# Seven block products for the second product of two token groups, and all weight operands kept in DRAM

## The chip, the cores and the metric

The kernel runs on one core of a Trainium2 chip. The metric is the device time of one execution in microseconds; the median of the runs is the figure to be predicted. TensorE is called PE here, VectorE DVE, ScalarE ACT, GpSimd POOL, and SyncE SP; SP issues nearly all DMAs. One execution was also profiled; its span runs from the first to the last instruction on the core.

## What is computed

Linear attention gives 2304 rows of 512 features. A gated feed-forward layer maps them to 2304 x 512 again. Then eight experts with router weights P (from eight rounds of row and column scaling of `exp(x @ w_gate)`) are summed, and this last stage is what the change touches:

```python
out = np.zeros((N, D), dtype=np.float32)
for e in range(E):
    h = np.maximum(x @ w1[e], 0.0)
    ye = h @ w2[e]
    out += P[:, e:e + 1] * ye
```

N is 2304, D 512, E 8, and h has 1024 columns for each expert. Everything is fp32. Each operand is split into a high part, rounded to the matmul's own type, and a low part (the rest); a product is then three matmuls: high by high, high by low, low by high.

## The kernel before

The last stage cuts the tokens into three groups of 768 (`GROUPS`), and each group into two halves of 384 (`NT`). For each group, the eight experts are worked off in four slices of 256 columns of h, so a group has 32 *units* and the stage 96. Unit n belongs to group 0, 1 or 2 in the code; in words these are groups one, two and three.

**First product of a unit** (`m2_burst`, `m2_m1`, `m2_product`, line 1162). The 256 x 512 slice of w1 and the 512 x 768 tokens are taken as 2 x 2 blocks, and Strassen's scheme in Winograd's form makes the four result blocks from seven block products, called M1 to M7 in the code (`PRODUCTS`). Its weight side needs A11, A12, A22 and four sums S1 to S4; its token side B11, B21, B22 and four sums T1 to T4. Each of the seven is six matmuls of 128 x 128 weights by 384 columns, so 42 in all. They run through two PSUM banks (`sbank`, tiles sb). DVE adds the pieces together (line 1238), ACT applies the relu and makes the high part (line 1176), DVE the low part (line 1179).

**Second product** (`m2_second`, `m2_s2`, lines 1192 to 1194). Here h is the weight side: for each of six token tiles of 128 there are six matmuls of 512 columns, 36 in all, summed over the four units of an expert in six PSUM banks (tiles yb). After the fourth unit `m2_evac` multiplies each bank by the router weight of its tokens and adds it to acc or accx (line 1211); after the last expert it stores the rows.

**Weights.** `load_unit` loads 512 KB of w1 and 512 KB of w2 for a unit (tiles rw). `prep` forms the four sums on DVE, and the high (ACT) and low (DVE) parts of the seven operands (tiles u, from the pool `wp` of nine slots), and those of w2. `prep_tick` does one step of that at a time, between the pieces of other work. For units 0 and 1 the finished operands are also written to DRAM (`keep`, tiles kept), and the first two units of the other groups read them back (`prep_kept`).

**Order.** Nothing schedules this work: each engine runs its instructions in the order in which the code issues them, and so does SP with its DMAs, each waiting at the queue's head for its semaphores. While a unit's second product runs, DVE prepares the next unit's weights; at the end of a group the functions called through `later` build the next group's token operands (`operands`, tiles op).

## Time and profile before

| what | us |
|---|---|
| median of 3 runs | 2058.14 |
| lowest and highest run | 2057.95, 2060.36 |
| span of the profiled execution | 2056.3 |
| PE busy | 2036.7 (99%) |
| DVE busy | 1328.5 (65%) |
| ACT busy | 821.1 (40%) |
| POOL busy | 142.8 (7%) |

The span is read with the busy shares only as a first look: matmuls are pipelined, so a busy PE says that it always has a matmul in flight, and not how fast they follow. The rhythm has to be taken from the start times. The last stage fills the time from about 556 us to the end.

### The profile page before, as it was taken

How to read it: one execution, taken by the hardware profiler on the slowest of the kernel's cores; microseconds unless marked ns; L12 is line 12 of the kernel's file. 1: busy time of each engine (PE TensorE's matmuls, PEld its weight loads, DVE VectorE, ACT ScalarE, POOL GpSimd, SP SyncE). 2: the span in 40 equal slices, each digit the busy share in tenths (PEclk: the TensorE clock that was granted, in tenths of full speed). 3: DMA queues.
4: the chain of work that ended last, by engine and by line, in shares of the span. 5: the costliest groups of instructions: out<-in, count | busy, mean ns of one | idle time of the engine just before them, and what ended most of it. 6: DMA issues, size and time to landing. Idle time of an engine off the chain costs nothing.

```text
span 2056.3 us, 26589 instructions
## 1 busy us (share of the span) xinstructions
PE 2036.7 (99%) x10391; PEld 1811.7 (88%) x10391; DVE 1328.5 (65%) x2660; ACT 821.1 (40%) x1603; POOL 142.8 (7%) x162
## 2 busy tenths in 40 slices
PE   8899999999999999999999999999999999999999
PEld 7788888887898999999899899899899989989988
DVE  7865753543678667667666667766666666666774
ACT  5644532322444434334334434433434533433442
POOL 4532211111100000000000000000000000000000
PEclk9999999999999999999999999999999999999999
DMA  9400310110222221221252222222134221122220
GB/s 270 127 24 21 103 53 30 52 58 10 77 72 63 82 62 62 74 70 62 69 177 62 65 80 62 66 79 62 62 107 139 62 81 63 62 74 70 62 71 32
DMA packets 108357, 153.24 MB, mean 75 GB/s; under 512 B 5832, under 2 KB 72392, under 8 KB 107464
## 3 DMA queue, kind: packets, MB, share of 16 engines
q1 hardware_dynamic: 107960, 151.43, 23.2%
q8 instruction: 81, 1.33, 0.3%
q14 instruction: 44, 0.36, 0.1%
q10 hardware_dynamic: 272, 0.13, 0.0%
HBM read 141.05 MB, written 10.49 MB: 74 GB/s over the span
## 4 chain that ended last, share of the span: by engine, by line
PE 96%; DVE 1%; POOL 0%; ACT 0%; issue 0%; DVEq 0%
PE sb L1162 34%; PE yb L1194 13%; PE yb L1193 13%; PE yb L1192 13%; PE pg L801 2%; PE y L803 2%; PE pv L801 2%; PE y L802 2%; PE y L801 2%; PE pg L802 2%; PE pg L803 2%; PE pv L802 2%; PE pv L803 2%; PE kv L458 1%; PE xp L543 1%; PE lg L894 0%
## 5 line engine op out<-in xcount | busy, mean ns | idle before, releaser
L1244 ACT COPY cs<-sb 128x384 f32<-128x384 f32 x96 | 46.1, 480 | 551.7 <-PE sb L1162 551.7
L1238 DVE TENSOR_TENSOR u<-mc,sb 128x384 f32<-128x384 f32 x96 | 53.1, 553 | 305.8 <-PE sb L1162 305.8
L1193 PE MATMUL yb<-u,hw 128*128 128x512 f32 x576 | 225.4, 391 | 0.0
L1194 PE MATMUL yb<-u,hw 128*128 128x512 f32 x576 | 225.2, 391 | 0.0
L1194 PE MATMUL yb<-u,hq 128*128 128x512 f32 x576 | 225.0, 391 | 0.0
L1193 PE MATMUL yb<-u,hq 128*128 128x512 f32 x576 | 224.5, 390 | 0.0
L1192 PE MATMUL yb<-u,hw 128*128 128x512 f32 x576 | 224.3, 389 | 0.0
L1192 PE MATMUL yb<-u,hq 128*128 128x512 f32 x576 | 223.9, 389 | 0.0
L1238 DVE TENSOR_TENSOR cs<-u,sb 128x384 f32<-128x384 f32 x288 | 159.1, 553 | 85.3 <-PE sb L1162 84.0
L1176 ACT ACTIVATE hq<-cs 128x384 fp32r<-128x384 f32 x192 | 100.9, 526 | 200.7 <-DVE cs L1238 200.7
L1162 PE MATMUL sb<-op0T,u 128*128 128x384 f32 x768 | 144.5, 336 | 0.4 <-DVE u L1238 0.4
L1162 PE MATMUL sb<-op2T,u 128*128 128x384 f32 x768 | 144.3, 335 | 0.0
L1162 PE MATMUL sb<-op1T,u 128*128 128x384 f32 x768 | 144.3, 335 | 0.0
L1162 PEld LDWEIGHTS sb<-op0T,u 128*128 128x128 f32 x768 | 134.8, 188 | 3.0 <-DVE u L1238 0.7
L1162 PEld LDWEIGHTS sb<-op2T,u 128*128 128x128 f32 x768 | 134.9, 188 | 2.5
L1162 PEld LDWEIGHTS sb<-op1T,u 128*128 128x128 f32 x768 | 134.9, 188 | 2.5
L1192 PEld LDWEIGHTS yb<-u,hq 128*128 128x128 f32 x576 | 108.2, 188 | 23.8
L1193 PEld LDWEIGHTS yb<-u,hq 128*128 128x128 f32 x576 | 108.0, 188 | 23.6
L1194 PEld LDWEIGHTS yb<-u,hw 128*128 128x128 f32 x576 | 108.1, 188 | 22.8
L1194 PEld LDWEIGHTS yb<-u,hq 128*128 128x128 f32 x576 | 108.1, 188 | 22.7 <-DVE hq L1179 0.4
L1069 DVE TENSOR_TENSOR u<-rw,u 128x512 fp32r<-128x512 f32 x184 | 125.5, 683 | 1.2 <-ACT u L1060 1.2
L1193 PEld LDWEIGHTS yb<-u,hw 128*128 128x128 f32 x576 | 108.1, 188 | 19.5
(244 smaller groups left out, 4151.4 us busy)
## 6 DMA issues: line engine op xcount, KB each, us to landing
rw<-in_moe_w_dram SPq DMA_DIRECT2D x184, 512.0 KB, 3.6
u<-kept SPq DMA_DIRECT2D x8, 896.0 KB, 4.6
raw<-in_moe_w_gate_dram SPq DMA_DIRECT2D x10, 512.0 KB, 3.7
raw<-in_moe_w_val_dram SPq DMA_DIRECT2D x10, 512.0 KB, 3.7
k<-in_k_dram SPq DMA_DIRECT2D x8, 512.0 KB, 5.2
acc<-in_q_dram SPq DMA_DIRECT2D x8, 512.0 KB, 8.6
v<-in_v_dram SPq DMA_DIRECT2D x16, 256.0 KB, 6.8
raw<-in_moe_w_out_dram SPq DMA_DIRECT2D x8, 512.0 KB, 3.5
```

The source lines that it names most:

```text
L458: nc.tensor.matmul(kv[:, (h - h0) * 2 * DV : (h - h0 + 1) * 2 * DV], lhsT=kk.rearrange("p c d -> p (c d)"), rhs=vv, start=(u == 0 and h == ...
L801: nc.tensor.matmul(o, lhsT=w(0), rhs=xb[0], start=first, stop=False)
L802: nc.tensor.matmul(o, lhsT=w(0), rhs=xb[1], start=False, stop=False)
L803: nc.tensor.matmul(o, lhsT=w(1), rhs=xb[0], start=False, stop=last)
L1069: tt(out=w2[:, 1, f], in0=r2[:, f], in1=w2[:, 0, f].bitcast(F32), op=ALU.subtract)
L1162: nc.tensor.matmul(bank[:, 0:NT], lhsT=w[wz][:, WI[wname], c, :], rhs=x[:, xz, c, :], start=(start and c == 0 and j == 0), stop=(c == 1 an ...
L1176: nc.scalar.activation(out=h[:, 0], in_=src, func=AF.Relu)
L1192: nc.tensor.matmul(py, lhsT=h[:, 0, s], rhs=w2[:, 0, f], start=(u == 0 and f == 0), stop=False)
L1193: nc.tensor.matmul(py, lhsT=h[:, 0, s], rhs=w2[:, 1, f], start=False, stop=False)
L1194: nc.tensor.matmul(py, lhsT=h[:, 1, s], rhs=w2[:, 0, f], start=False, stop=(u == UE - 1 and f == 1))
L1238: add = lambda o, a, b: nc.vector.tensor_tensor(out=o, in0=a, in1=b, op=ALU.add)
L1244: nc.scalar.copy(out=c11, in_=px)
```

## The change

Group one keeps its form, with its seven first products in another order (M1, M2, M6, M5, M7, M4, M3), two of the sums replaced by ACT copies out of PSUM, and two of the six second-product tiles run inside the next unit's first product. `prep` becomes `prep_first` (w1) and `prep_second`, which now also forms the sums of w2's blocks and seven operands of them. Every unit of group one writes all its operands to DRAM (`keep`: 4 x 896 KB), and the units of groups two and three only read them back (`recall`).

In groups two and three the second product is made by seven block products as well, and transposed: w2 is the weight side, and the result has 128 features by 384 tokens. The router weight must then be in h. So `probs_out` writes P, transposed, to DRAM, `probs_in` reads an expert's row back, broadcast to all partitions (`pb0`, or a part of acc1), and `half_mul` does relu and product in one DVE instruction. `m2_p1(n)` is the first product of unit n and `m2_p2(n - 1)`, called after it, the second product of the unit before. A block is three matmuls of 384 columns. M2, M3 and M4 stay in the six banks yb over a whole group (`m2_stay`); M1, M5, M6 and M7 go in turn through the two banks sb (`m2_turn`), and DVE adds each into SBUF (`m2_fold`, tiles in acc0 and acc1). The differences T1 to T4 of h (`sum_of`) and the low parts (`lo`) wait in a list, `pend`, from which `pop` issues them at fixed places. `m2_p2_last` closes a group: it adds the products together, PE transposes 24 blocks back (`turned_part`), and `turned_out` stores the rows.

At the end of group one the operands of group two are built as before; at the end of group two those of group three are built inside `m2_p2(62)` and `m2_p2_last(63)`, with their sums on POOL.

The core of the diff:

```diff
+    def keep(n, k, pair):
+
+        for z, t in enumerate(pair):
+            kept[n, k, z] = d = dp.tile([P, KW], F32, name=f"kept{n}_{k}_{z}")
+            t = t.bitcast(F32)
+            if k == 0:
+                nc.sync.dma_start(out=d, in_=t[:, 0:KW])
+            else:
+                nc.sync.dma_start(out=d[:, 0 : 2 * P], in_=t[:, 0 : 2 * P])
+                nc.sync.dma_start(out=d[:, 2 * P : KW], in_=t[:, 4 * P : 2048])
...
+    def recall(n, k):
...
+        pair = slots(f"u{n}_{k}")
+        for z, t in enumerate(pair):
+            nc.sync.dma_start(out=t[:, 0:KW].bitcast(F32), in_=kept[n % PER, k, z])
+        if k == 0:
+            w1s[n] = first_view(pair)
+        else:
+            w2s[n] = pair
...
+    def prep_second(n):
+
+        r2 = unit_raw.pop((n, 1)).rearrange("p f e -> p (f e)")
+        a11, a21, a12, a22 = (r2[:, z * 256 : (z + 1) * 256] for z in range(4))
+        sums = sp.tile([P, 1024], I32, tag="raw", name=f"t{n}", bufs=RAWS).bitcast(F32)
+        s1, s2, s3, s4 = (sums[:, z * 256 : (z + 1) * 256] for z in range(4))
+        pair = w2s[n] = slots(f"u{n}_1")
+        hi, lo = pair
...
+        tt(out=s3, in0=a11, in1=a21, op=ALU.subtract)
+        tt(out=s4, in0=a12, in1=s2, op=ALU.subtract)
+        cp(out=hi[:, 1024:1536], in_=sums[:, 0:512])
+        yield
+        tt(out=lo[:, 0:1024], in0=r2, in1=hi[:, 0:1024].bitcast(F32), op=ALU.subtract)
+        cp(out=hi[:, 1536:2048], in_=sums[:, 512:1024])
+        yield
+        tt(out=lo[:, 1024:1536], in0=sums[:, 0:512], in1=hi[:, 1024:1536].bitcast(F32), op=ALU.subtract)
+        yield
+        tt(out=lo[:, 1536:2048], in0=sums[:, 512:1024], in1=hi[:, 1536:2048].bitcast(F32), op=ALU.subtract)
+        keep(n, 1, pair)
+
...
-        m2_product(n, "M5", x, True)
-        add(c22, u2, px)
-        low22 = m2_relu(n, 1, 1, c22)
-        low11()
+        m2_product(n, "M5", y, True)
+        m2_low(0, 0, c11)
         mid(2)
-        m2_product(n, "M4", y, False)
-        add(c21, u1, py)
-        low21 = m2_relu(n, 1, 0, c21)
+        m2_product(n, "M7", x, False)
+        nc.scalar.copy(out=u2, in_=px)
         mid(3)
-        m2_product(n, "M3", x, False)
-        add(c12, u1, px)
-        low12 = m2_relu(n, 0, 1, c12)
-        low21()
+        add(c22, u2, py)
+        m2_relu(1, 1, c22)
+        m2_product(n, "M4", x, False)
+        nc.scalar.copy(out=c21, in_=px)
+        m2_low(1, 1, c22)
+        m2_relu(1, 0, c21)
         mid(4)
-        low12()
-        low22()
-
...
+    def probs_in(g, e):
...
+            return
+        t = pb_place[(g * E + e) % 2]
+        d = state["pd"].rearrange("(t e) p -> t e p", e=E)
...
+            src = d[4 * b + j : 4 * b + j + n, e, :]
+            nc.sync.dma_start(
+                out=t[:, at * P : (at + n) * P].rearrange("p (t q) -> p t q", t=n), in_=src.partition_broadcast(P)
+            )
...
+    def half_mul(n, name, c):
+        g, e, u = units[n]
+        z = int(name[2]) - 1
+        nc.vector.scalar_tensor_tensor(
+            out=fb[name],
+            in0=c,
+            scalar=0.0,
+            in1=pbc[g, e][:, z * NT : (z + 1) * NT],
+            op0=ALU.max,
+            op1=ALU.mult,
+        )
+
+    def hi(n, name):
+        nc.scalar.copy(out=hop[n][name][:, 0], in_=fb[name])
+
+    def lo(n, name):
+        h = hop[n][name]
+        nc.vector.tensor_tensor(out=h[:, 1], in0=fb[name], in1=h[:, 0].bitcast(F32), op=ALU.subtract)
+
+    def sum_of(n, name):
+        x, y = {"T1": ("B12", "B11"), "T2": ("B22", "T1"), "T3": ("B22", "B12"), "T4": ("B21", "T2")}[name]
+        nc.vector.tensor_tensor(out=fb[name], in0=fb[x], in1=fb[y], op=ALU.subtract)
+        hi(n, name)
+
+    pend = []
...
+    def m2_p1(n):
+
+        old = ring["old"]
...
+        add = lambda o, a, b: nc.vector.tensor_tensor(out=o, in0=a, in1=b, op=ALU.add)
+        m1, u1 = mt[:2]
+        m5 = m1
+        m2_product(n, "M1", x, True)
+        nc.scalar.copy(out=m1, in_=px)
+        pop(2)
+        m2_product(n, "M2", y, True)
+        pop(1)
+        m2_product(n, "M6", x, False)
+        add(fb["B11"], m1, py)
+        nc.scalar.copy(out=u1, in_=px)
+        half_mul(n, "B11", fb["B11"])
+        m2_product(n, "M5", y, True)
+        nc.scalar.copy(out=m5, in_=py)
+        hi(n, "B11")
+        pop(2)
+        m2_product(n, "M7", x, False)
+        pop(len(pend))
+        add(fb["B22"], m5, px)
+        half_mul(n, "B22", fb["B22"])
+        hi(n, "B22")
+        m2_product(n, "M3", y, False)
+        m2_product(n, "M4", x, False)
+        add(fb["B12"], u1, py)
+        half_mul(n, "B12", fb["B12"])
+        half_mul(n, "B21", px)
+        hi(n, "B21")
+        for name in ("T3", "T1", "T2", "T4"):
+            pend.append(lambda name=name: sum_of(n, name))
+        for name in ("B11", "B22", "B21", "T1", "T2", "T3", "T4"):
+            pend.append(lambda name=name: lo(n, name))
+
...
+    def m2_mm(n, name, j, bank, start):
+
+        wname, hname = PRODUCTS[name]
+        w, h = w2s[n], hop[n][hname]
+        d = slice(WI[wname] * 2 * P + j * P, WI[wname] * 2 * P + (j + 1) * P)
+        for k, (wz, hz) in enumerate(((0, 0), (0, 1), (1, 0))):
+            nc.tensor.matmul(
+                bank[:, 0:NT], lhsT=w[wz][:, d], rhs=h[:, hz], start=(start and k == 0), stop=True, skip_group_check=True
+            )
...
+    def m2_stay(n, name, j):
+        m2_mm(n, name, j, ybank[2 * ("M2", "M3", "M4").index(name) + j], n % PER == 0)
...
+    def m2_turn(n, name, j, bank):
+        m2_mm(n, name, j, bank, True)
+
+    def m2_fold(n, name, j, bank):
+        a = macc[name, j]
+        if n % PER == 0:
+            nc.vector.tensor_copy(out=a, in_=bank[:, 0:NT])
+        else:
+            nc.vector.tensor_tensor(out=a, in0=bank[:, 0:NT], in1=a, op=ALU.add)
...
+    def m2_p2(n, work):
+
+        y, x = sbank
+        m2_stay(n, "M3", 0)
+        m2_turn(n, "M1", 0, x)
+        m2_stay(n, "M2", 0)
+        m2_turn(n, "M1", 1, y)
+        m2_fold(n, "M1", 0, x)
+        m2_stay(n, "M2", 1)
+        pop()
+        m2_turn(n, "M5", 0, x)
+        m2_fold(n, "M1", 1, y)
+        pop()
+        work(0)
+        m2_turn(n, "M5", 1, y)
+        m2_fold(n, "M5", 0, x)
+        m2_stay(n, "M4", 0)
+        pop()
+        m2_turn(n, "M6", 0, x)
+        m2_fold(n, "M5", 1, y)
+        work(1)
+        m2_turn(n, "M6", 1, y)
+        m2_fold(n, "M6", 0, x)
+        pop()
+        work(2)
+        m2_stay(n, "M3", 1)
+        m2_turn(n, "M7", 0, x)
+        m2_fold(n, "M6", 1, y)
+        m2_turn(n, "M7", 1, y)
+        m2_fold(n, "M7", 0, x)
+        work(3)
+        m2_stay(n, "M4", 1)
+        m2_fold(n, "M7", 1, y)
...
+    def m2_p2_last(n, work, later):
...
+        for k, m in ((1, 2), (6, 2), (5, 3), (7, 3)):
+            name = f"M{k}"
+            m2_turn(n, name, 0, x)
+            m2_turn(n, name, 1, y)
+            m2_stay(n, f"M{m}", int(k in (6, 7)))
+            for j, bank in ((0, x), (1, y)):
+                m2_fold(n, name, j, bank)
+            for j in range(2):
+                if k == 6:
+                    add(A(6, j), A(1, j), A(6, j))
+                elif k == 5:
+                    add(A(5, j), A(5, j), A(6, j))
+                elif k == 7:
+                    add(A(6, j), A(6, j), A(7, j))
+                    add(A(7, j), A(7, j), A(5, j))
             work(k)
-            if k % 2:
-                next(state["steps"], None)
+        finals = [lambda z=z, k=k, j=j: add(A(k, j), R(z, j), A(k, j)) for z, k in ((2, 1), (3, 5), (4, 6)) for j in range(2)]
+        if later:
+            pend.extend(finals)
+        else:
+            for f in finals[0:4]:
+                f()
+        m2_stay(n, "M4", 0)
+        m2_stay(n, "M4", 1)
+        if not later:
+            for f in finals[4:6]:
+                f()
+            for i in range(3, 6):
+                turned_part(i, 1, 1, rows_bank[i])
+
...
+    def turned_out(g, i, ps, eng):
+
+        b, j = gtiles[g][i]
+        o = [acc[2], acc[3]][i // 4][:, i % 4, :]
+        eng(out=o, in_=ps)
+        nc.sync.dma_start(out=out_rows(b, j), in_=o)
...
+    pb_place = [pb0[:, 0 : 2 * NT], flat[1][:, 3 * NT : 5 * NT]]
+    probs_in(1, 0)
...
+    ORDER2 = ["oB11", "oB21", "T1", "oT1", "T2", "oT2", "oT3", "T4", "oT4", "oB22"]
+    later = operands(2, ORDER2, temp2, lambda name: mt[int(name[-1])])
...
+    for n in range(PER, last + 1):
+        g, e, u = units[n]
+        start = n % PER == 0
+        if u == 1:
+            probs_in(*((g, e + 1) if e < E - 1 else (g + 1, 0)))
+        if start and g > 1:
+            m2_p2(n - 2, lambda k: (flush(k), next(later)))
+            m2_p2_last(n - 1, lambda k: [next(later, None) for _ in range(2)], True)
+            assert next(later, None) is None
+            m2_p1(n)
+            for i in range(6):
+                for d in range(2):
+                    turned_part(i, d, i // 3, ybank[i])
+                turned_out(g - 1, i, ybank[i], nc.vector.tensor_copy if i % 3 == 1 else nc.scalar.copy)
+            pop(6)
+        elif start:
+            m2_p1(n)
+            pop(6)
+        else:
+            m2_p1(n)
+            if not (g < len(GROUPS) - 1 and n % PER == PER - 1):
+                m2_p2(n - 1, flush if n == last else idle)
+        recall(n + 2, 0)
+        recall(n + 1, 1)
+    rows_bank = [ybank[0], ybank[1], ybank[3], sbank[0], sbank[1], ybank[2]]
```

**Where instructions stand: DVE in the steady unit of group two or three.** Before, at the end of unit 39, the preparation of unit 41's weights stands in a row with the evacuations of an expert of group two (s and u are weight tiles, rw the loaded weights, yb the PSUM banks):

```order
L1049 TENSOR_TENSOR s41_9683<-rw41_0_9564,s41_9683 128x256 [waits DVE_49]
L1211 SCALAR_TENSOR_TENSOR acc1_106<-yb0_4814,probs_104,acc1_106 128x512 [waits PE_49]
L1052 TENSOR_TENSOR u41_1_9681<-rw41_0_9564,u41_0_9680 128x512 [waits Activation_49]
L1211 SCALAR_TENSOR_TENSOR acc1_106<-yb1_4815,probs_104,acc1_106 128x512 [waits PE_49]
L1055 TENSOR_TENSOR u41_1_9681<-rw41_0_9564,u41_0_9680 128x256 [waits Activation_49]
L1211 SCALAR_TENSOR_TENSOR accx_4820<-yb2_4816,probs_104,accx_4820 128x512 [waits PE_49]
```

After, in the second product of a unit of group three (acc0 and acc1 hold the folded products, sb the two PSUM banks, mt2, acc4 and fy1 the differences T3, T1 and T2, T4 of h; L1408 is the fold and L1330 the difference):

```order
L1408 TENSOR_TENSOR acc0_105<-sb0_4674,acc0_105 128x384 [waits PE_49]
L1330 TENSOR_TENSOR mt2_9362<-fx_9356,fy1_9358 128x384 [waits DVE_49]
L1408 TENSOR_TENSOR acc0_105<-sb1_4675,acc0_105 128x384 [waits PE_49]
L1330 TENSOR_TENSOR acc4_109<-fy1_9358,fx_9356 128x384
L1408 TENSOR_TENSOR acc0_105<-sb0_4674,acc0_105 128x384 [waits PE_49]
L1330 TENSOR_TENSOR acc4_109<-fx_9356,acc4_109 128x384 [waits DVE_49]
L1408 TENSOR_TENSOR acc0_105<-sb1_4675,acc0_105 128x384 [waits PE_49]
L1408 TENSOR_TENSOR acc0_105<-sb0_4674,acc0_105 128x384 [waits PE_49]
L1330 TENSOR_TENSOR fy1_9358<-fy0_9357,acc4_109 128x384 [waits DVE_49]
L1408 TENSOR_TENSOR acc1_106<-sb1_4675,acc1_106 128x384 [waits PE_49]
L1408 TENSOR_TENSOR acc1_106<-sb0_4674,acc1_106 128x384 [waits PE_49]
L1408 TENSOR_TENSOR acc1_106<-sb1_4675,acc1_106 128x384 [waits PE_49]
```

The weights have left DVE; eight folds stand there now, with the four differences set between them.

**Where instructions stand: SP at the end of group one.** Before, the operands of unit 33 (u, from kept) are read back around the first stores of the group:

```order
L1006 DMA u33_0_8697<-kept1_0_4708 128x1792 [waits DMAHW3_49,PE_49]
L1007 DMA u33_1_8698<-kept1_1_4710 128x1792 [waits DVE_49,PE_49]
L995 DMA rw34_0_8701<-in_moe2_w1_dram 128x4x256 [waits DMAHW5_49,DVE_49]
L995 DMA rw34_1_8703<-in_moe2_w2_dram 128x2x512 [waits DMAHW7_49,DMAHW6_49,DVE_49]
L1219 DMA out_0_dram<-acc0_105 128x512 [waits DVE_49]
L1219 DMA out_0_dram<-acc0_105 128x512 [waits DMAHW0_49,DVE_49]
L1013 DMA u33_2_8764<-kept1_2_4712 128x2048 [waits DMAHW1_49,PE_49,Pool_49]
```

After, the last two of the group's six stores, two operand pairs, and the router weights of group two (pd is P in DRAM, pb0 its place in SBUF):

```order
L1226 DMA out_0_dram<-accx_4828 128x512 [waits DMAHW2_49,DVE_49]
L1226 DMA out_0_dram<-accx_4828 128x512 [waits DMAHW3_49,DVE_49]
L1016 DMA u32_1_0_9339<-kept0_1_0_4630 128x1792 [waits DMAHW4_49,PE_49]
L1016 DMA u32_1_1_9340<-kept0_1_1_4633 128x1792 [waits DMAHW5_49,PE_49]
L1016 DMA u33_0_0_9343<-kept1_0_0_4808 128x1792 [waits DMAHW6_49,PE_49]
L1016 DMA u33_0_1_9344<-kept1_0_1_4810 128x1792 [waits DMAHW7_49,PE_49,Pool_49]
L1303 DMA pb0_9359<-pd_7227 128x2x128 [waits DMAHW3_49,DMAHW2_49,DMAHW0_49]
L1303 DMA pb0_9359<-pd_7227 128x128 [waits DMAHW1_49]
```

The read of the router weights now stands behind the six stores and four reads of 896 KB, and it is what DVE's first product of group two needs.

**Where instructions stand: DVE at the end of group two.** Before, in unit 63, the operands of group three (op2) stand between the evacuations:

```order
L1114 TENSOR_TENSOR op2B21_12606<-acc2_107,op2B21_12606 128x2x256 [waits Activation_49]
L1114 TENSOR_TENSOR op2B21_12606<-acc3_108,op2B21_12606 128x2x128 [waits Activation_49]
L1211 SCALAR_TENSOR_TENSOR acc1_106<-yb0_4814,probs_104,acc1_106 128x512 [waits PE_49]
L1114 TENSOR_TENSOR op2T3_12619<-t2T3_12498,op2T3_12619 128x768 [waits Activation_49]
L1211 SCALAR_TENSOR_TENSOR acc1_106<-yb1_4815,probs_104,acc1_106 128x512 [waits PE_49]
L1114 TENSOR_TENSOR op2T1_12630<-long0_4821,op2T1_12630 128x768 [waits Activation_49]
```

After, in the last two second products of group two, between the folds, with their sums made by POOL:

```order
L1326 TENSOR_TENSOR hb_9348<-mt2_9362,hb_9348 128x384
L1326 TENSOR_TENSOR hb_9348<-fy1_9358,hb_9348 128x384 [waits Activation_49]
L1408 TENSOR_TENSOR acc1_106<-sb0_4674,acc1_106 128x384 [waits PE_49]
L1408 TENSOR_TENSOR acc1_106<-sb1_4675,acc1_106 128x384 [waits PE_49]
L1116 TENSOR_TENSOR op2T1_13453<-acc2_107,op2T1_13453 128x2x256 [waits Activation_49]
L1116 TENSOR_TENSOR op2T1_13453<-acc2_107,op2T1_13453 128x2x128 [waits Activation_49]
L1408 TENSOR_TENSOR acc1_106<-sb0_4674,acc1_106 128x384 [waits PE_49]
L1408 TENSOR_TENSOR acc0_105<-sb1_4675,acc0_105 128x384 [waits PE_49]
L1408 TENSOR_TENSOR acc0_105<-sb0_4674,acc0_105 128x384 [waits PE_49]
L1116 TENSOR_TENSOR op2T2_13475<-acc2_107,op2T2_13475 128x2x256 [waits Activation_49]
L1116 TENSOR_TENSOR op2T2_13475<-acc2_107,op2T2_13475 128x2x128 [waits Activation_49]
L1408 TENSOR_TENSOR acc0_105<-sb1_4675,acc0_105 128x384 [waits PE_49]
```

The operand copies now stand among folds of the two banks through which PE turns.

## Rows read from the trace of the kernel before

**Rows 1.** The core's span, us, and its mean granted TensorE clock

```profile
core 0: 2056.3 us, clock 0.999
```

**Rows 2.** The page's chain that ended last: share of the span by engine

```profile
PE 96%; DVE 1%; POOL 0%; ACT 0%; issue 0%; DVEq 0%
```

**Rows 3.** That chain's pieces in time: start us, us, engine, tile, line, instructions

```profile
609.18 7.30 PE sb L1162 x42
...
1043.76 7.30 PE sb L1162 x42
...
1075.28 7.30 PE sb L1162 x42
```

**Rows 4.** Waits: engine line <- waited for: us in all, times, longest us

```profile
PE sb L1162 <- DVE cs L1238: 0.4, 2, 0.2
```

**Rows 5.** DVE in time, 900 to 914: start us, us, line, op, out<-in, [idle before<-releaser]

```profile
900.02 0.69 DVE L1062 TENSOR_TENSOR u<-s,u 128x512 fp32r<-128x512 f32 x1
900.63 0.68 DVE L1069 TENSOR_TENSOR u<-rw,u 128x512 fp32r<-128x512 f32 x1
...
908.35 0.55 DVE L1238 TENSOR_TENSOR cs<-u,sb 128x384 f32<-128x384 f32 x1 [0.49 <-PE sb L1162]
908.82 0.55 DVE L1179 SCALAR_TENSOR_TENSOR hw<-cs,hw 128x384 fp32r<-128x384 f32 x1
...
912.52 0.42 DVE L1044 TENSOR_TENSOR s<-rw 128x256 f32<-128x256 f32 x1
912.97 0.42 DVE L1045 TENSOR_TENSOR s<-s,rw 128x256 f32<-128x256 f32 x1
913.32 0.42 DVE L1048 TENSOR_TENSOR s<-rw 128x256 f32<-128x256 f32 x1
```

**Rows 6.** PE and DVE in time, near 563 and 905, in the same columns

```profile
562.55 0.55 DVE L1238 TENSOR_TENSOR u<-mc,sb 128x384 f32<-128x384 f32 x1
...
563.15 3.42 PE L1162 MATMUL sb<-op0T,u 128*128 128x384 f32 x18 [0.36 <-DVE u L1238]
...
905.03 1.20 PE L1162 MATMUL sb<-op0B,u 128*128 128x384 f32 x6
905.23 0.55 DVE L1238 TENSOR_TENSOR u<-mc,sb 128x384 f32<-128x384 f32 x1 [3.92 <-PE sb L1162]
```

**Rows 7.** Page, groups by line: busy us, mean ns | idle before, its releaser

```profile
L1244 ACT COPY cs<-sb 128x384 f32<-128x384 f32 x96 | 46.1, 480 | 551.7 <-PE sb L1162 551.7
...
L1238 DVE TENSOR_TENSOR cs<-u,sb 128x384 f32<-128x384 f32 x288 | 159.1, 553 | 85.3 <-PE sb L1162 84.0
...
L1162 PEld LDWEIGHTS sb<-op0T,u 128*128 128x128 f32 x768 | 134.8, 188 | 3.0 <-DVE u L1238 0.7
```

**Rows 8.** Stretches: us, busy by engine (instructions), granted clock, DMA share, GB/s

```profile
core 0: us, PE busy (x) PEld busy (x) DVE busy (x) ACT busy (x) POOL busy (x), PEclk, DMA share, GB/s
453.00:460.00 7.00, 7.00 (x33) 5.79 (x32) 4.04 (x8) 1.79 (x4) 1.30 (x1) 1.00 0.88 330
1030.00:1032.00 2.00, 2.00 (x14) 2.00 (x13) 1.06 (x2) 1.00 (x2) 0.00 (x0) 1.00 0.90 369
```

**Rows 9.** DMA issues: out<-in, queue, count, KB each, median us to landing

```profile
u<-kept SPq DMA_DIRECT2D x8, 896.0 KB, 4.6
...
acc<-in_q_dram SPq DMA_DIRECT2D x8, 512.0 KB, 8.6
...
out_dram<-accx SPq DMA_DIRECT2D x6, 256.0 KB, 3.0
```

**Rows 10.** DVE and SP in time, the last 7 us

```profile
2052.27 0.75 DVE L1211 SCALAR_TENSOR_TENSOR acc<-yb,probs,acc 128x512 f32<-128x512 f32 x1 [0.61 <-PE yb L1194]
...
2053.05 0.33 SPq L1219 DMA_DIRECT2D out_dram<-acc  x1
```

**Rows 11.** Groups by line and shape, POOL and PE

```profile
L841 POOL TENSOR_TENSOR h<-th,h 128x512 fp32r<-128x512 f32 x48 | 63.3, 1319 | 278.3 <-ACT h L840 278.3
...
L796 PE MATMUL cold<-ident 128*128 128x128 f32 x67 | 7.8, 273 | 0.0
```

More of the change, by code (lines that the diff above doesn't have):

```diff
@@ L978 @@
     gtiles = [gtiles[2 * g] + gtiles[2 * g + 1] for g in range(len(GROUPS))]
-    KEPT = 2
-    kept = {}
+    tt, cp = nc.vector.tensor_tensor, nc.scalar.copy
     def load_unit(n, k):
-        if n >= len(units) or units[n][0] and n % (E * UE) < KEPT:
+        if n >= PER:
             return
@@ L1086, in prep_all, with prep_until @@
+    todo = [(prep_first, prep_second)[k](n) for n in range(PER) for k in range(2)]
+    state["items"] = state["prepared"] = 0
+    def prep_tick():
+        k = state["prepared"]
+        if k < min(state["items"], len(todo)) and next(todo[k], todo) is todo:
+            state["prepared"] += 1
+    def prep_until(k):
+        while state["prepared"] < min(k, len(todo)):
             prep_tick()
@@ L1384 @@
         state["made"] += 1
-    while "first" not in state:
-        prep_tick()
+    prep_until(1)
     sbank = [psum(f"sb{z}") for z in range(2)]
@@ new lines, with slot, mid @@
+    later = operands(1, ORDER, temp1, None)
+    evacs = []
+    def slot():
+        while evacs:
+            if evacs.pop(0)():
+                return
+        prep_tick()
+    for n in range(PER):
+        end = n == PER - 1
+        if n:
+            def mid(k, n=n):
+                if k in (1, 3):
+                    slot()
+                    m2_s2(n - 1, 4 + k // 2)
+                    evacs.append(lambda: m2_evac(n - 1, 4 + k // 2))
+                    if k == 3:
+                        state["items"] = 2 * n + 4
+                slot()
+                if k in (0, 2) and n == PER - 1:
+                    next(later)
+                if k == 4:
+                    next(steps, None)
+            m2_burst(n, mid)
+            if not end:
+                prep_until(2 * n + 3)
+                m2_m1(n + 1)
+        state["items"] = 2 * n + 5
+        if n == PER - 2:
+            prep_until(2 * PER)
+        slot()
+        for k in range(6 if end else 4):
+            m2_s2(n, k)
+            evacs.append(lambda n=n, k=k: m2_evac(n, k))
+            slot()
+            if n >= PER - 2:
+                next(later, None)
+            if k in (0, 2):
+                next(steps, None)
+        if end:
+            while evacs:
+                evacs.pop(0)()
+        if n == PER // 2:
+            probs_out()
+        if n == PER - 2:
+            recall(PER, 0)
```

322 lines of the change are left out of this document (169 added, 153 removed).

## The prediction

> **What bounds the kernel now.** I read the core's span first [rows 1]: one core, TensorE's granted clock 0.999, which is its upper level of 2.4 GHz; nothing is lost to the clock. The chain that ended last is 96% PE [rows 2], so time can only go where PE does less or waits more. The pieces of that chain in order of time show the rhythm of the last stage [rows 3]: each of the 96 units opens with one piece of 42 matmuls of 384 columns (the first product) that takes 7.30 us, or 7.30/42 = 0.174 us a matmul. From 609.18 to 1043.76 are 28 units, 15.52 us each; that leaves 8.2 us for the 36 matmuls of 512 columns of the second product, 0.228 us each. From 1043.76 to 1075.28 are two units with the change from group one to group two between: 31.52, so that change costs 0.5. In the list of waits the largest entry of PE in this stage is 0.4 us in all [rows 4]: PE is fed without a gap.
>
> Second, what an operation of DVE really takes. In the groups by line a 384-column add lasts 553 ns [rows 7]; in the order of time [rows 5] the next, independent one starts 0.47 after it (908.35, 908.82), a 512-column one 0.60 after (900.02, 900.63), a 256-column one 0.35 after (912.97, 913.32); one that needs the result of the one before it starts 0.45 after instead of 0.35 (912.52, 912.97), 0.1 more. So a full DVE queue is priced at 0.47 per 384 columns, and 0.57 where an operation needs its neighbour. The hand-overs come from [rows 6]: PE's next block starts at 905.03 and DVE's add on the finished one at 905.23, a lag of 0.20; back, DVE's add of 0.55 begun at 562.55 lets PE go at 563.15, so 0.05 after it ends.
>
> **What is removed.** The second product of groups two and three becomes 14 blocks of three matmuls of 384 columns: 42 x 0.174 = 7.3 instead of 8.2, so 0.91 a unit and **58.2 us** for 64 units. The operand shapes and the hi, hi, lo order of the weights are the first product's, so I take its rate. The bound above: the weight loads last 188 ns each [rows 7]; were they not overlapped as now, 42 x 0.188 = 7.9 and two thirds of the gain gone (38 us). The same loads run in the first product at 0.174, so I do not take it. The weight preparation of DVE and ACT in those groups goes too, worth nothing directly, since PE did not wait for it.
>
> **The steady unit of groups two and three.** DVE gets 26 operations of 384 columns a unit: 7 in the first product (three adds, four products with the router weight), 4 differences, 7 low parts, 8 folds of turned blocks. 26 x 0.47 + 3 x 0.1 = 12.5 us against 14.6 of PE: it fits, at 86%. But only two PSUM banks turn, so PE can wait on single folds. By hand, blocks of 7.3/14 = 0.521 from the start of the second product: M5's first block is done at 3.13, its fold starts at 3.33; the difference T2 stands next in the queue (3.80), then the fold of M5's second block (4.27), which ends at 4.82. PE wants that bank for M6's second block at 9 x 0.521 = 4.69 and gets it at 4.87: **0.18 lost**. All other hand-overs hold: in the first product the adds end 0.2 before PE needs the bank, the fold for M7's second block ends at 6.43 against 6.44. So 14.78 a unit; 60 units of this form, 60 x 0.18 = **10.8 us**. Bounds: 0 if the difference finds a gap, and the 0.56 of the first rival below. ACT has ten operations of about 0.5 [rows 7], five of 14.6 us, and hides.
>
> **Group one.** It keeps its 78 matmuls. DVE loses two adds a unit to ACT and gains four sums and 1024 columns of low part for the second weights: about 12 of 15.5 us, under PE's cover; in the new order the tightest place I find is the add for C22, ready near 6.9 where PE wants the bank at 7.9. Every unit now writes 4 x 0.875 MiB to DRAM and reads 1 MiB: 4.7 MB per 15.5 us = 304 GB/s. Groups two and three read 3.67 MB per 14.8 us = 248 GB/s. The trace has carried more: 330 GB/s over 7 us at a DMA share of 0.88 while kept operands were written, 369 at 0.90 while they were read, with PE busy all the time [rows 8]. So I take 0; bounds, 0 and, at the 248 GB/s of 3.67 MB in 14.8, some 3.5 us a unit. At the stage's start eight preparation steps stand ahead of DVE's first add (four sums, two low parts and the last evacuations of the stage before): about **1 us**, 0 to 2.
>
> **From group one to two: 8 us.** In SP's new order the six output stores come first, then two kept operand pairs (u32_1 and u33_0, 3.67 MB), and only then the broadcast of the router weights for group two (pb0), which also waits for the two accx stores. DVE's last evacuations lie between the operand copies (from 1.6: six of 0.66, the 0.75 of [rows 10] less the overlap, and five copies of 0.95, so 10.3 against PE's 8.2) and end some 2.2 after PE; the last is issued at 2.3 and lands 3.0 later [rows 9], so pb0 is released at 5.3; but the 3.67 MB issued from 2.7 on take 9 us at 369/0.90 = 410 GB/s [rows 8], until 12, and loads issued in a crowd land late (the first q loads 8.6 us, a lone kept load 4.6 [rows 9]), so I put its landing at 13. DVE's product with pb0 waits there, and behind it, in DVE's queue, the add that frees the bank for PE's M4, due at 6.3: 13 + 0.57 + 0.55 + 0.05 = 14.2. Lost 7.9, less the 0.5 paid now: **7.5**. Bounds: 4.3 if pb0 lands 4.6 after its release, 13 if the pairs move at 248 GB/s.
>
> **From group two to three: 14.5 us.** The operands of group three can only be written when group two's first products are over, so DVE does them inside the last two second products. From the start of P2(62) to the fold that frees a bank for P1(64) it has 16 folds, 4 differences, 7 low parts, 4 adds (31 x 0.47 = 14.6), six operand steps of 512 + 256 columns (6 x 0.95 = 5.7), T3 (2.6), and one wait for POOL's T2 (512 columns last 1.32 there [rows 11], so 2.0 for 768, and ACT's copy behind it: 2.4). Sum 25.3 against PE's 14.6: 10.7. Then six adds delay P1(64)'s first evacuation by 1.3, and 24 transposes at 7.8/67 = 0.117 [rows 11] add 2.8. Together 14.9, less 0.5. Bounds 8 to 19: these are queue lengths, and a wait on POOL can hide or repeat.
>
> **The end: 9.4 us.** Now the last evacuation starts at 2052.27 and the last store is issued at 2053.05; the span ends 4.1 after PE [rows 10, 1]. Then: seven low parts (3.3) stand ahead of a fold in P2(94) and hold PE by 3.2; from the start of P2(94) PE's last block ends at 18.3, DVE's closing adds at 23.1, the transposes of M6 follow at 23.9, copies at 24.9, store 3.2: 28.1. Without a wait it would be 14.6 + 4.1 = 18.7. Bounds 5 to 12.
>
> **The sum**, against the profiled span of 2056.3: -58.2 + 10.8 + 0 + 1 + 7.5 + 14.5 + 9.4 = -15.0, so 2041.3. The median of the runs, 2058.14, is 1.8 above the span, which I add: **2043 us**, 0.7% faster.
>
> **The rivals.** (1) *DVE at full length, slower.* The Trainium skill speaks for it: VectorE: DVE Perf Modes, section Terms, says of DRAIN "Pipeline flush emitted after every DVE op; next op can't issue until 8-slice pipe empties". Row 908.82 disagrees: it starts 0.08 before the end of the operation at 908.35. As a mechanism of this kernel: if folds that read PSUM and rewrite their own sum follow each other only after their full 0.553, a unit has 14.4 us of DVE plus forced waits, and the same hand schedule gives 0.56 lost a unit, 33.6 in all; the transitions grow to 38. Then -58.2 + 33.6 + 38 = +13.4, or 2071. It turns slower from 0.42 a unit. For it: no row shows a fold in place. Against it: rows 908.35 and 908.82, where the first reads PSUM. (2) *DMA as the bound*: group one at 3.5 us a unit more, 2043 + 31 x 3.5 = 2151; against it stand the rates above. (3) *The gain isn't there*: 0.188 a matmul, 2043 + 38 = 2081. (4) *Better covered transitions*: at their lower bounds (4 + 8 + 5 - 1) and no wait in the unit, -58.2 + 16 = -42, 2016; at half of that, 2026.
>
> **How the numbers follow.** My forecast, 2043 with 2032 to 2054 of its own from the bounds of the transitions, 0.62; (4) 0.18; (1) 0.12; (2) and (3) 0.04 each. About 0.2% (4 us) can be told from no change by a measurement. Faster by more: (4) and nine tenths of the forecast, 0.74. Slower: (1) to (3), 0.20 less a little of (1), 0.19. Same: 0.07. The range goes down to 2024, where half of (4) is inside, and up to 2072 to take in (1): outside stay (2), (3) and part of (4), under 0.2.
>
> **What the profile after would show.** A unit of groups two and three at 14.8 us with one short PE wait on the fold line; DVE starts 0.47 apart; group one still 15.5; one PE wait of about 8 us near 1065 in the first product on an add of DVE that itself stood behind a DMA; some 11 us of PE waits on folds near 1540; the last store about 13 us after PE's last matmul block. Wrong would be: DVE starts 0.55 apart, a unit at or over 15.0, DMA at a share near 1 in group one, or a granted clock below 0.99.

## The result: slower by 1.1%, and the profile after

The changed kernel takes 2080.94 us (median of four runs, 2080.86 to 2081.74) against 2058.05 for the kernel before: a ratio of 1.0111, 95% interval 1.0097 to 1.0126. The prediction was 2043, with a range to 2072. The forecast sign is wrong, and the size by 38 us.

The core's span and granted clock, where [rows 1] had 2056.3 and 0.999:

```profile
core 0: 2078.9 us, clock 0.992
```

The page's chain by engine, where [rows 2] had 96% PE:

```profile
PE 89%; DVE 5%; ACT 1%; DMA 1%; issue 1%; POOL 0%; SPq 0%; ACTq 0%; DVEq 0%
```

The chain in order of time (start, us, what), where the pieces of [rows 3] were PE's, 15.52 apart:

```profile
1072.94 3.63 DMA out_dram<-accx
1078.46 11.81 DMA pb<-pd
...
1109.50 7.29 PE sb L1167 x42
1124.36 7.29 PE sb L1167 x42
...
1557.35 1.87 DVE hd L1326 x4
...
1568.30 1.32 DVE acc L1447 x2
...
1950.88 7.31 PE sb L1167 x42
1965.82 7.31 PE sb L1167 x42
```

The steady unit of groups two and three is what was forecast, 14.87 (14.93 in part of group three) against 15.51. The new pieces are the places where the chain leaves PE: two DMAs near 1075, DVE near 1557 and 1568. To price them I cut the last stage at the ends of the second products of units 31 and 63 and compared the two traces stretch by stretch. The kernel before has already run M1 of the next unit by then, six matmuls; at both cuts their 1.04 us are taken off its time:

| stretch | forecast, us against before | measured |
|---|---|---|
| group one | +1 | +12.7 |
| group two, with both changes of group | -5.5 | +10.1 |
| group three, with the end | -10.6 | -0.2 |
| sum | -15.1 | +22.6 |

So every stretch missed, by 11.7, 15.6 and 10.4. Below, "lost" is the time between the starts of two matmuls beyond the 0.174 (384 columns) or 0.228 (512) of an unhindered pair.

**Group one.** A view of two stretches (us, then busy time and instruction count of PE, PEld, DVE, ACT, POOL, granted clock, DMA share, GB/s). Before, PE made 688 matmuls from 583 to 720 and 1612 from 720 to 1040:

```profile
583.00:720.00 137.00, 137.00 (x688) 123.75 (x687) 102.54 (x234) 60.73 (x118) 4.08 (x7) 1.00 0.22 70
720.00:1040.00 320.00, 320.00 (x1612) 290.26 (x1611) 216.81 (x426) 125.80 (x248) 0.00 (x0) 1.00 0.23 73
```

After:

```profile
583.00:720.00 137.00, 133.48 (x658) 117.63 (x657) 113.37 (x257) 74.08 (x142) 3.88 (x8) 1.00 0.80 289
720.00:1040.00 320.00, 318.21 (x1587) 285.71 (x1587) 248.21 (x481) 155.14 (x305) 0.00 (x0) 1.00 0.82 302
```

30 and 25 matmuls fewer, at 15.51/78 = 0.199 each: 6.0 and 5.0 us. DVE is busy 83% and 78% of the time there. What stands in its queue ahead of one late add (DVE and PE in order of time; ca, probs and the cs of L938 are the router's row and column scaling, the cs of L1242 is a block of h, t and s are sums of weights, u weight operands):

```profile
640.79 0.43 DVE L938 TENSOR_REDUCE cs<-probs 128x8 f32<-128x144 f32 x1
641.35 1.23 DVE L1069 TENSOR_TENSOR u<-rw,u 128x1024 fp32r<-128x1024 f32 x1
642.50 0.68 DVE L1072 TENSOR_TENSOR u<-t,u 128x512 fp32r<-128x512 f32 x1
...
643.53 0.31 DVE L944 SCALAR_TENSOR_TENSOR probs<-probs,ca 128x144 f32<-128x144 f32 x1
...
645.28 0.55 DVE L1242 TENSOR_TENSOR cs<-mc,sb 128x384 f32<-128x384 f32 x1
645.88 1.31 PE L1167 MATMUL sb<-op0T,u 128*128 128x384 f32 x6 [1.14 <-DVE cs L1242]
```

**From group one to two.** DVE's product with pb waits for the DMA, PE for DVE:

```profile
1088.06 0.56 DVE L1312 SCALAR_TENSOR_TENSOR fx<-fx,pb 128x384 f32<-128x384 f32 x1 [14.34 <-DMA pb<-pd]
1089.14 2.29 PE L1167 MATMUL sb<-op1T,u 128*128 128x384 f32 x6 [11.90 <-DVE fx L1355]
```

The six matmuls behind the wait take 2.29 us instead of 1.2: the granted clock has fallen to half. The same happens in four more places, three of them shown here and the fourth from 2058.5 to 2061.9. In the view of stretches (the granted clock is the third number from the end):

```profile
1089.20:1092.40 3.20, 3.15 (x9) 2.64 (x10) 1.97 (x5) 0.51 (x1) 0.00 (x0) 0.50 1.00 404
1561.20:1566.80 5.60, 5.60 (x18) 5.60 (x19) 3.81 (x8) 1.02 (x2) 2.26 (x3) 0.50 0.48 164
1573.60:1577.10 3.50, 3.50 (x12) 3.50 (x13) 3.50 (x8) 0.48 (x2) 0.00 (x0) 0.52 0.00 0
1594.30:1597.60 3.30, 3.30 (x11) 3.30 (x11) 1.26 (x3) 0.89 (x2) 0.00 (x0) 0.50 1.01 326
```

**The steady unit** still holds one wait. PE and DVE (sb are the two turning banks, L1408 the fold, L1330 the difference T2); the six matmuls of M6 take 1.49 instead of the 1.21 of M7's:

```profile
1313.21 0.56 DVE L1408 TENSOR_TENSOR acc<-sb,acc 128x384 f32<-128x384 f32 x1
1313.68 0.55 DVE L1330 TENSOR_TENSOR acc<-fx,acc 128x384 f32<-128x384 f32 x1
1314.15 1.18 DVE L1408 TENSOR_TENSOR acc<-sb,acc 128x384 f32<-128x384 f32 x2
...
1314.05 1.49 PE L1393 MATMUL sb<-hd,u 128*128 128x384 f32 x6
...
1315.90 1.21 PE L1393 MATMUL sb<-hd,u 128*128 128x384 f32 x6
```

### The profile page after: what moved, and what is told of

The parts are those of the page before. It is cut to its first block, busy times and chain, and to the rows that moved or that the text cites. A ratio compares the mean times of both kernels' runs of the same rounds, so it can differ in the third digit from the quotient of the medians.

```text
span 2078.9 us, 29053 instructions
## 1 busy us (share of the span) xinstructions
PE 2019.9 (97%) x10825; PEld 1853.4 (89%) x10825; DVE 1592.4 (77%) x3198; ACT 809.7 (39%) x1603; POOL 149.1 (7%) x168
## 4 chain that ended last, share of the span: by engine, by line
PE 89%; DVE 5%; ACT 1%; DMA 1%; issue 1%; POOL 0%; SPq 0%; ACTq 0%; DVEq 0%
PE sb L1167 32%; PE sb L1393 13%; PE yb L1393 9%; PE yb L1202 4%; PE yb L1201 4%; PE yb L1200 4%; PE pg L801 2%; PE pv L801 2%; PE y L803 2%; PE pg L802 2%; PE pg L803 2%; PE pv L802 2%; PE pv L803 2%; PE y L802 2%; PE y L801 2%; PE kv L458 1%
## 5 line engine op out<-in xcount | busy, mean ns | idle before, releaser
L1408 DVE TENSOR_TENSOR acc<-sb,acc 128x384 f32<-128x384 f32 x496 | 273.1, 555 | 56.5 <-PE sb L1393 50.0
L1167 PEld LDWEIGHTS sb<-op1T,u 128*128 128x128 f32 x768 | 134.7, 189 | 14.7 <-DVE fx L1355 13.1
L1393 PE MATMUL sb<-hc,u 128*128 128x384 f32 x516 | 113.9, 342 | 6.3 <-DVE acc L1408 5.9
L1393 PE MATMUL sb<-hd,u 128*128 128x384 f32 x504 | 111.3, 342 | 3.4 <-DVE acc L1408 3.0
L1167 PE MATMUL sb<-op0B,u 128*128 128x384 f32 x576 | 112.2, 338 | 2.3 <-DVE cs L1242 1.8
L1167 PE MATMUL sb<-op1B,u 128*128 128x384 f32 x576 | 110.8, 335 | 0.0
L1167 PE MATMUL sb<-op2B,u 128*128 128x384 f32 x576 | 110.3, 334 | 0.0
L1167 PEld LDWEIGHTS sb<-op0B,u 128*128 128x128 f32 x576 | 101.2, 188 | 7.1 <-DVE cs L1242 3.7
L1393 PEld LDWEIGHTS sb<-hc,u 128*128 128x128 f32 x516 | 89.7, 189 | 15.1 <-DVE acc L1408 14.0
L1393 PE MATMUL yb<-hd,u 128*128 128x384 f32 x444 | 102.4, 338 | 0.0
L1167 PEld LDWEIGHTS sb<-op1B,u 128*128 128x128 f32 x576 | 101.2, 189 | 0.6 <-DVE fy L1355 0.6
L1167 PEld LDWEIGHTS sb<-op2B,u 128*128 128x128 f32 x576 | 100.9, 188 | 0.0
L1393 PEld LDWEIGHTS sb<-hd,u 128*128 128x128 f32 x504 | 88.1, 189 | 11.2 <-DVE acc L1408 10.1
```

What stands on the lines that cost most here:

```text
L1167: nc.tensor.matmul(bank[:, 0:NT], lhsT=w[wz][:, WI[wname], c, :], rhs=x[:, xz, c, :], start=(start and c == 0 and j == 0), stop=(c == 1 an ...
L1393: nc.tensor.matmul(bank[:, 0:NT], lhsT=w[wz][:, d], rhs=h[:, hz], start=(start and k == 0), stop=True, skip_group_check=True)
L1408: nc.vector.tensor_tensor(out=a, in0=bank[:, 0:NT], in1=a, op=ALU.add)
```

## The experiments

All start from the changed kernel; its 2080.9 us from the runs above is the mark, and the kernel before ran beside each at 2057.8 to 2058.0.

**One difference behind a fold** (in `m2_p2`).

```diff
-        pop()
         m2_turn(n, "M6", 0, x)
         m2_fold(n, "M5", 1, y)
+        pop()
         work(1)
```

> One edit to the changed kernel: in the second product of a unit of groups two and three the third difference (T2) is issued behind the fold of M5's second block instead of ahead of it. Theory A (order in DVE's queue): PE's wait of 0.18 in each unit, and the 0.11 that its first matmul after a wait takes longer, go: 14.87 becomes 14.59 a unit, 60 x 0.28 = 17, so 2064 us. Theory B (DVE is too full there, at 77% busy on the whole): the wait moves to the next fold, M6's second block, and the unit stays within 0.1 of 14.87, 2078 to 2081 us.

Measured: 2081.44 (2080.83 to 2082.87), units of 14.89. The M6 piece is clean now and the M7 piece has the wait, since T4 stands ahead of the fold that frees its bank:

```profile
1288.20 1.20 PE L1393 MATMUL sb<-hc,u 128*128 128x384 f32 x6
...
1289.76 1.51 PE L1393 MATMUL sb<-hc,u 128*128 128x384 f32 x6
```

Theory B was right about the wait moving on; whether DVE is too full is the next question.

**Both differences behind folds.** T4 is issued after the last fold.

```diff
         m2_fold(n, "M6", 0, x)
-        pop()
         work(2)
...
         m2_fold(n, "M7", 1, y)
+        pop()
```

> The changed kernel with two differences moved in the second product of a unit of groups two and three: T2 behind the fold of M5's second block, and T4 behind the last fold (M7's second block). After the first edit alone the wait stood at M7's second block, whose bank is freed by the fold ahead of which T4 stood. Theory A (only the order counts): no wait is left, 14.6 a unit, 60 x 0.28 = 17, so 2064 us. Theory B (DVE is too full, the wait goes on moving, into the next first product): 14.85 to 14.9 a unit, 2080 us.

Measured: 2061.9 (ten runs, 2060.7 to 2063.4), 19 us less. The chain's pieces stand 14.57 apart, which is 84 x 0.1735, no wait at all:

```profile
1182.96 7.29 PE sb L1167 x42
1197.52 7.29 PE sb L1167 x42
```

DVE is as full as before, so only the order counted. 0.30 a unit went, of which the wait itself was 0.18; the first matmul after it starts its successor 0.11 later than usual.

**The router weights of group two early.** They go into the spare columns of two token operands, and the read is issued, with the operands of units 32 and 33, ahead of the stores.

```diff
             m2_burst(n, mid)
+            if end:
+                recall(PER, 1)
+                recall(PER + 1, 0)
+                probs_in(1, 0)
...
-        t = pb_place[(g * E + e) % 2]
+        if (g, e) == (1, 0):
+            t = [spare[1, "B11"], spare[1, "T2"]]
```

> One place of the changed kernel: the router weights of group two's first expert go into spare columns of two token operands instead of accx's place, so that their read no longer waits for accx's stores, and the two kept operand pairs and this read are issued ahead of group one's stores. Theory A (the wait of 12 us is that DMA alone, and the half clock and the two smaller waits behind it come from it): some 13 of the 16 us lost between groups one and two go, 2068 us, and no half clock near 1090. Theory B (the next thing is late there anyway, the operands of unit 33 or DVE's queue): PE waits 5 or more us a little later, 2076 us or more, and the half clock stays.

Measured: 2067.46 (2064.84 to 2068.69), 13.5 less. The first product of unit 32 runs through:

```profile
1070.74 2.27 PE L1170 MATMUL sb<-op1B,u 128*128 128x384 f32 x12
1072.85 3.28 PE L1170 MATMUL sb<-op1T,u 128*128 128x384 f32 x18
1075.97 1.20 PE L1170 MATMUL sb<-op1B,u 128*128 128x384 f32 x6
1077.01 1.21 PE L1170 MATMUL sb<-op1T,u 128*128 128x384 f32 x6
```

The half clock near 1090 is gone too, and about 3 us of waits on ACT and DVE stay. In the view of stretches:

```profile
1089.20:1092.40 3.20, 3.20 (x21) 3.20 (x20) 2.94 (x6) 1.39 (x3) 0.00 (x0) 1.00 0.98 296
```

Theory A. The edit does two things, it issues the read earlier and gives it a place that waits for no store; their shares were not separated.

**One round of the router's scaling instead of eight** (`ITERS = 1`).

> The changed kernel with one round of the router's row and column scaling instead of eight (seven rounds are left out, so the router weights differ). These rounds run on DVE and POOL during units 2 to 9 of group one. Theory A (DVE's queue is what PE waits for in group one, and the rounds fill it up): the 6.0 us that PE loses between 583 and 720 fall to 1 or less; 2075 us. Theory B (the writes of the kept operands to DRAM, near 300 GB/s, delay the loads there): no change, 2080 to 2082.

Measured: 2078.45 (2075.83 to 2079.82). Its first stretch:

```profile
583.00:720.00 137.00, 136.48 (x682) 122.61 (x681) 104.17 (x208) 75.23 (x145) 0.43 (x1) 1.00 0.82 303
```

682 matmuls instead of 658: 24 x 0.199 = 4.8 of the 6.0 us come back in the place that theory A named. Only 2.5 us reach the median. In its trace 2.4 us are lost before the last stage begins, where the edit changes nothing (its first matmul starts at 558.41 instead of 556.01), and group two is 1.8 longer, with units of 14.87 to 14.93 and a few 0.3 longer still, for a reason that I did not find.

**No writes of kept operands but those of two units.**

```diff
+        if n > 1:
+            return
         for z, t in enumerate(pair):
...
-            nc.sync.dma_start(out=t[:, 0:KW].bitcast(F32), in_=kept[n % PER, k, z])
+            nc.sync.dma_start(out=t[:, 0:KW].bitcast(F32), in_=kept[n % 2, k, z])
```

> The changed kernel that writes only the operands of the first two units of group one to DRAM; all units of groups two and three read those (so they compute with the wrong weights). It takes away 3.67 MB of DMA writes from each of 30 units of group one. Theory A (group one loses its 12.5 us to the order and the length of DVE's queue): no change there, units of 15.57 and 16.1, 2080 to 2082. Theory B (DMA traffic delays loads, or DVE's and ACT's accesses): the units fall to 15.51, 2070 to 2076.

Measured: 2080.49, no change, with 65 GB/s in group one instead of 289:

```profile
583.00:720.00 137.00, 133.71 (x659) 117.77 (x658) 113.56 (x257) 74.17 (x142) 4.79 (x8) 1.00 0.21 65
720.00:1040.00 320.00, 318.21 (x1587) 285.70 (x1586) 248.33 (x480) 155.08 (x305) 0.00 (x0) 1.00 0.22 67
```

Traffic is not what group one pays for.

**The sums of the weight blocks on POOL.** Eight `tt(out=s...)` become `nc.gpsimd.tensor_tensor`.

> The changed kernel with the eight sums of a unit's weight blocks in group one made on POOL instead of DVE. Theory A (DVE's queue): DVE is relieved of 8 x 0.35 = 2.8 us a unit; the losses in units 2 to 9 (6.5) and the 0.54 of every fourth unit (7 x 0.54 = 3.8) go, 2071 us. Theory B (DMA): no change, 2081. Theory C (POOL takes about 0.8 us for each, and DVE's low parts now wait for it through ACT): slower, 2085 or more.

Measured: 2163.05 (2158.73 to 2165.68), far worse than theory C. POOL in order of time, while the router's scaling runs:

```profile
593.05 0.73 POOL L1062 TENSOR_TENSOR t<-t,rw 128x256 f32<-128x256 f32 x1
601.83 0.42 POOL L940 PARTITION_ALL_REDUCE ca<-cs  x1 [8.05 <-issue]
609.47 0.71 POOL L1065 TENSOR_TENSOR t<-rw 128x256 f32<-128x256 f32 x1 [7.21 <-issue]
```

Each change between a sum and the all-reduce costs POOL 6 to 8 us, nearly always with no wait that the profile shows. Units 1 to 6 become 19 to 39 us long. After the last round, units are 15.57 and every fourth 16.1, as without the edit: relieving DVE by 2.8 us a unit did not touch that loss of 0.54.

**The low parts of h on POOL** (`lo` with `nc.gpsimd`).

> The changed kernel with the seven low parts of a unit's h in groups two and three made on POOL instead of DVE. Theory A (DVE's queue is what PE waits for in the last two second products of groups two and three): the waits of 3.6 us behind six low parts near 1561 and of 3.2 near 2057 go, with their half clock: 6 to 9 us, 2072 to 2075; the steady unit keeps its 0.28, because that one comes from a difference. Theory B (POOL, at some 1.0 us a low part, is late, or slows DVE beside it): the unit grows over 14.9, DVE's folds start more than 0.47 apart, 2085 or more.

Measured: 2157.38 (2155.34 to 2158.35), units of 16.2. Theory B, but not by POOL being late: from 1200 to 1500 PE waits for DVE's folds and never for POOL. DVE's groups from 1200 to 1500 here, and one of the kernel with both differences moved, where POOL is idle:

```profile
L1408 DVE TENSOR_TENSOR acc<-sb,acc 128x384 f32<-128x384 f32 x151 | 81.4, 549 | 13.8 <-PE sb L1393 12.3
L1330 DVE TENSOR_TENSOR mt<-fx,fy 128x384 f32<-128x384 f32 x19 | 26.3, 1384 | 0.0
L1330 DVE TENSOR_TENSOR fy<-fy,acc 128x384 f32<-128x384 f32 x19 | 23.4, 1233 | 0.0
```

```profile
L1330 DVE TENSOR_TENSOR mt<-fx,fy 128x384 f32<-128x384 f32 x21 | 11.5, 548 | 0.0
```

The differences that meet a POOL operation take 1384 and 1233 ns instead of 548; the folds, with one input in PSUM, stay at 549. The Trainium skill states this (SBUF — State Buffer, section "Who interferes with whom"): a DVE instruction with two SBUF inputs contends with a GpSimd instruction that reads SBUF, one with at most one SBUF input, outside the 2-port perf modes, doesn't. These rows agree.

**Group three without its own token operands.** `X2[2] = X2[1]`, and no operand steps.

> The changed kernel without the token operands of group three (that work is left out, group three computes with group two's operands). Of the 20.6 us that PE loses between 1538 and 1600: theory A (the operand steps on DVE are what the folds wait for, as in the prediction's sum): 8 to 10 go, about 2071 us. Theory B (the six low parts ahead of one fold, and the clock behind, are most of it): 5 or less go, 2076 or more.

Measured: 2067.8 (2067.03 and 2068.58), 13.1 less. One long wait is left between 1540 and 1580, the one behind six low parts:

```profile
1557.63 1.12 PE L1393 MATMUL sb<-hc,u 128*128 128x384 f32 x3 [3.02 <-DVE acc L1408]
```

Theory A, and by more than it said: between the starts of units 63 and 66 it is 11.9 of the 20.6, the operand steps with their share of the half clock.

**Small matmuls in the two long waits.** 26 and 29 transposes ahead of M7's second block in `m2_p2(62)` and of M7 in `m2_p2_last(63)`; the sum that is kept in their bank is lost by it.

```diff
+        for _ in range(k if n == m else 0):
+            nc.tensor.transpose(ybank[0][:, NT : NT + P], ident, ident)
```

> The changed kernel with 26 and 29 transposes of 128 columns (0.117 us each, into columns of a bank that nobody reads) put into the two long waits of PE near 1558 and 1570, between groups two and three. The waits stay. Theory A (the granted clock falls because PE waits, and the half clock costs by itself): the clock stays at 1.0 from 1555 to 1600 and the 0.15 more of some 30 matmuls there go, 3 to 5 us, 2076 to 2078. Theory B (DVE sets the pace there, a slower PE costs nothing): 2080 to 2082, or more by what the transposes overrun.

Measured: 2077.04 (2076.31 to 2077.92), 3.9 less. The clock stays up, and the wait of 3.42 us is filled:

```profile
1557.86 3.00 PE L1412 MATMUL yb<-ident 128*128 128x128 f32 x26
1561.44 0.79 PE L1393 MATMUL sb<-hc,u 128*128 128x384 f32 x3 [0.58 <-DVE acc L1408]
```

```profile
1561.20:1566.80 5.60, 5.33 (x27) 4.71 (x28) 5.27 (x12) 1.03 (x2) 3.51 (x4) 1.00 0.57 200
1573.60:1577.10 3.50, 2.66 (x16) 2.34 (x15) 3.46 (x8) 0.00 (x0) 0.00 (x0) 1.00 0.00 0
```

Theory A: the half clock behind a wait has its own price here.

**Everything together, with the low parts on POOL,** and with the sixth evacuation of group one behind the add for C22:

```diff
                         state["items"] = 2 * n + 4
-                slot()
+                if k != 3 or units[n - 1][2] < UE - 1:
+                    slot()
```

> All repairs in one: both differences moved, the router weights of the first expert read early into spare columns, the low parts of groups two and three on POOL, and the evacuation of the sixth tile in group one issued behind the add for C22 instead of ahead of it. If theory A holds throughout: 2081 - 17 - 13.5 - 7 - 7 x 0.54 = 2040 us, 0.9% faster than the kernel before. If the low parts on POOL are late: 2060 or more.

Measured: 2108.51 (2107.1 to 2110.2): the low parts on POOL stretch the unit to 15.67. The evacuation's place did what it was meant for: units of 16.1 have become 15.57.

**The three repairs without POOL.**

> The changed kernel with three repairs together: both differences moved behind folds, the first expert's router weights read early into spare columns with the kept operands ahead of the stores, and the sixth evacuation of group one behind the add for C22. The low parts stay on DVE. Theory A (the losses lie apart from each other and add up): 2081 - 19 - 13.5 - 4 = 2044 us, 2040 to 2047, 0.7% faster than the kernel before. Theory B (one repaired wait is taken over by the next): two thirds of the gains at most, 2056 us or more.

Measured: 2043.9 (2042.15 to 2044.01), a ratio of 0.9928 to the kernel before, interval 0.9916 to 0.9941: theory A, the losses add up. The version is 0.7% faster than the kernel before. That its time is close to the forecast of 2043 is chance: its steady unit has no wait, and between the starts of units 63 and 66 it still loses about as much as the changed kernel (65.33 us for the three, against 66.94).

```profile
core 0: 2042.1 us, clock 0.995
```

From 720 to 1040 PE makes 1602 matmuls, 15 more than in the changed kernel: 15 x 0.199 = 3.0 us for the evacuation's place.

```profile
720.00:1040.00 320.00, 319.50 (x1602) 288.43 (x1601) 250.38 (x484) 156.77 (x306) 0.00 (x0) 1.00 0.82 305
```

**The repairs, and the waits filled** (with 30 matmuls in each, added into unread columns).

> The kernel with the three repairs, and 30 small matmuls of 128 columns added into unread columns of a bank in each of the two long waits between groups two and three. Theory A (the half clock behind a wait has a price of its own): the clock stays at 1.0 there, 3 to 4 us less than the same kernel without them. Theory B: no difference, or slower by what they overrun.

Measured: 2043.65 (2041.74 to 2046.16; ratio 0.9932, 0.9918 to 0.9945): no difference that can be told. In its trace the half clock between the groups is gone and the stretch from unit 63 to unit 66 is 1.5 us shorter, but the waits behind it grew. What filling is worth there stays open.

## Why the prediction was wrong, point by point

Every term for a wait was too small: group one by 11.7 us, the steady unit by some 8, the two changes of group by some 8 each, the end by 3. The first failed as a step, since it was put at nothing; the others had the right mechanism and the wrong size, and none of them had the clock. The sums themselves hold but for 0.1 and 0.2 us (7.9 - 0.5 is 7.4, and 10.7 + 1.3 + 2.8 - 0.5 is 14.3); the 2026 of rival (4) can't be followed from the figures beside it.

- **"58.2 us" for the second product: right.** With no wait left the unit is 14.57, 0.94 below 15.51. The third rival (0.188 a matmul) fell.
- **"0.18 lost" in the steady unit: the wait right, the term too small.** Place, fold and 0.18 are as worked out by hand. But the first matmul behind a wait costs 0.11 more, so 0.29, and some units of group three were 0.06 longer still: 18 to 19 us instead of 10.8. The first rival fell: DVE's starts stay 0.47 apart around the folds (1313.21, 1313.68, 1314.15), and two in a row take 1.01 us together (1560.55), against the Trainium skill's sentence on DRAIN that I quoted.
- **"Group one ... So I take 0": failed, 12.7 against 1.** The step was "about 12 of 15.5 us, under PE's cover". A share of busy time does not say that each hand-over is in time, and the sum left out DVE work that is in group one only: the rounds of the router's scaling, hidden before, of which seven cost 4.8 now. The "tightest place", the add for C22, was named rightly, but I did not see the evacuation of every fourth unit, which waits for PE's last tile, right ahead of it: 3.0. About 1.0 is the read-out of the router weights and 0.9 the stage's start, as forecast; some 3 us I did not trace further (15.57 instead of 15.51 in nearly every unit is 1.9 of them). The DMA half of the step was right: without the writes nothing changes.
- **"From group one to two: 8 us", with its term of 7.5: mechanism right, 16.3 lost instead of 7.9.** I landed pb0 at 13 after PE's end, and it landed at 17.3 (1088.06, with group one's last matmul ending at 1070.8), its second part 2.3 later. Its release was right, SP issues it at 1076.65, 5.8 after PE's end against 5.3; the read was mis-sized, 11.4 us instead of 7.7. My prices were those of large reads [rows 9]; this read is a broadcast to all partitions. Why it takes so long is not shown, but its median over the stage is 8.0 from issue to landing, in the list of DMA issues after (count, KB each, median us to landing):

```profile
pb<-pd SPq DMA_DIRECT2D x16, 128.0 KB, 8.0
```

- **"From group two to three: 14.5": mechanism right, 20.0 of waits and half clock instead of 12.0,** beside the 2.8 of transposes. The queue lengths were near: 15.1 before unit 64, of which 4.4 is the clock (29 matmuls, 0.15 more each), against 10.7. That the rest is 10.7 too is in part luck: in place of one wait of 2.4 on POOL and ACT, DVE has four short ones on ACT between 1551 and 1573, 2.95 in all. Behind it come 4.9 more against 1.3, in waits on ACT's copies and a third stretch of half clock.
- **"The end: 9.4": 12.** The 3.2 behind the seven low parts came as forecast (3.17). Of the 3 more, some 1.5 is again half clock (ten matmuls), and 1.7 the stores: the span ends 4.9 behind the last copy instead of 3.2.
- **What was left out of every term: the clock.** "Nothing is lost to the clock" was true of the kernel before, and I forecast waits of 8 and 11 us without asking what they do to it. Each long wait of PE was followed by matmuls at 0.32 instead of 0.174. Summed over the five stretches that is some 9 us of the 38 (58 matmuls, 0.15 more each); the filled waits of the changed kernel show 3.9 of them by themselves, those of the repaired one nothing that can be told.
- **The rivals.** None was it. The slower case that I priced (DVE at full length) was the wrong mechanism; what came was my own list of waits, each too small, with the clock on top and group one left out. Rival (3) priced 2081, and that the measured time is the same is chance: its matmuls at 0.188 did not come. None of my signs of being wrong came either (a unit of 14.87, a clock of 0.992, DVE starts 0.47 apart, a DMA share of 0.82 in group one): they watched the rivals and not the length of my own waits.
